# Attention: transposing the row maxima and the sums as 64-row products on both halves of TensorE, into two shared PSUM banks

## Chip, cores, metric

One core of one Trainium2 chip runs the whole program. The metric is the device time of one execution in microseconds; the shown times are medians of several executions.

## The reference

Two layers A (sliding-window attention) and two layers B (a spectral filter: 2-D FFT, a product with complex weights, inverse FFT), in the order A, B, A, B, each on a layer-normalised input and with its residual added. The change lies in A alone:

```python
def _A_ref(x, wqkv, wo):            # x is (1, 2048, 576)
    B, S, D = x.shape
    H = 32; Dh = D // H; W = 256    # 32 heads of 18
    ...                             # q, k, v from x @ wqkv, per head
    scores = jnp.einsum("bhqd,bhkd->bhqk", q, k) * (Dh ** -0.5)
    idx = jnp.arange(S)
    mask = (idx[:, None] - idx[None, :] >= 0) & (idx[:, None] - idx[None, :] < W)
    scores = jnp.where(mask[None, None], scores, -1e9)
    p = _softmax(scores, axis=-1)
    o = jnp.einsum("bhqk,bhkd->bhqd", p, v)
    return (lambda x, *d: x.transpose(*d))(o, 0, 2, 1, 3).reshape(B, S, D) @ wo
```

Each query sees itself and the 255 keys before it. All values are 32-bit floats.

## The kernel before

The instructions of each engine run in the order in which the Python code issues them; semaphores between the engines are placed by the library from the tiles that instructions read and write.

Attention handles the 32 heads in 8 groups of 4 (`NQ = 8`), and the 2048 positions in 16 tiles of 128. A step `t` of the main loop (from -10 to 129 in each layer) is one tile of one group. `qs` and `ks_` hold the queries and keys of a group transposed: two heads (`hp`) in partitions 0 to 63 and 64 to 127, two more (`pair`) in a second plane. Row 63 of each half of `qs` holds minus the maximum of that query, against a row of ones in `ks_`, so that the product of all 64 rows gives score minus maximum.

- `score_max(x, pair, hp)`, ten steps ahead (`LEAD = 10`): PE multiplies 63 rows of q and k into a bank `S` (L811); DVE adds the mask and takes the maximum of each query into a column of `ms` (L813).
- `m_rows(n, c)`, once in four steps (t = 4k + 2): PE transposes the 16 columns of maxima of four tiles (L819, bank `tpm`), ACT negates them into `mt` (L821), and four DMAs on the queue of SP put them into row 63 of `qs`.
- `exps(x, pair, hp)`: PE multiplies 64 rows of k and q into a bank `E` (L843), ACT takes the exponential into `P` (L844), POOL cuts the window's edges (L846, L849).
- `pv(x)`, two steps behind: PE multiplies `P` with v, which has a nineteenth column of ones, into `U` (L863): 19 rows for each head, starting at partitions 0, 32, 64 and 96, the last of them the sum of the exponentials. After four tiles ACT copies `U` to `us` (L868).
- `norm(n, c)`, in the same steps as `m_rows` and right behind it: PE transposes the four 128-column blocks of `us` into one bank `tpo` (L873), DVE takes the reciprocals of the sums (L876) and multiplies (L878) into `o`, which a DMA stores.
- `proj` makes q and k of later groups from the input, 14 pairs of 64-row products of 512 columns for each block of 128 rows and 512 positions (L750), one of a pair on each half of the array, spread over the steps; ACT copies one result (L758), DVE adds the other (L762).

In a step PE's order is: E, E, S, S (first `pair`), the products of `pv`, E, E, S, S (second `pair`), some products of `proj`, and in every fourth step `m_rows` and `norm`.

PSUM has eight banks: `U`, two for `proj`, and five for all else. `bank(name)` gives those five: a counter `turns` runs over the calls from t = 0 on, and its value modulo 5 decides between tag `S` (three banks: 1, 2, 0) and tag `E` (two banks: 3, 4). A new tile can be written once the readers of an earlier tile in the same bank are done. Before t = 0 only tag `S` is used.

After attention the object `out` multiplies with `wo`. There a tile `tpl` of one bank is used in slices of 128 columns, one for each tile of positions: `turn_last` transposes into a slice (L511), `split_last` reads it with ACT (L516) and then with DVE (L517). Slices 0, 1, 2 are written together and read in turn; later slice 3 is written and read, and then slice 0 is written again.

Of the kernel before, what the change touches and what calls it, by code (L numbers as in the profile page):

```python
# [8 lines left out]
F32 = mybir.dt.float32  # L9
F32R = mybir.dt.float32r  # L10
BF = mybir.dt.bfloat16
AF = mybir.ActivationFunctionType
# [563 lines left out]
def layer_a(tc, src, dst, wqk_d, wv_d, wo_d, dc_d, gc_d, dram, copy, wvs, wos, second, spectral):  # L576
    nc = tc.nc
    V, A, T, P = nc.vector, nc.scalar, nc.tensor, nc.gpsimd
# [7 lines left out]
    with ExitStack() as ctx:  # L586
        cp = ctx.enter_context(tc.tile_pool(name="ac", bufs=1))
        ident = cp.tile([128, 128], F32, name="ident")
# [127 lines left out]
        with ExitStack() as c2:  # L716
            wp = c2.enter_context(tc.tile_pool(name="a2", bufs=2))
# [56 lines left out]
            def bank(name):  # L774

                turns[0] += t >= 0
                return pp.tile([128, 512], F32, name=name, **(dict(tag="E", bufs=2) if turns[0] % 5 > 2 else dict(tag="S", bufs=3)))
# [3 lines left out]
            def stack_load(n, c):  # L781

                q, k = qs[n % 2], ks_[n % 2]
                cs = slice(c * 512, c * 512 + 512)
                for which, t, parts in ((0, q, (0, 0, 1)), (1, k, (0, 1, 0))):
                    for hp in range(2):
                        r0 = 144 * n + 72 * which + 36 * hp
                        for slot, part in enumerate(parts):
                            b = 64 * hp + 18 * slot
                            nc.sync.dma_start(t[b:b + 18, :, cs].bitcast(F32),  # L790
                                              qk_d[part, r0:r0 + 36, cs].rearrange("(f d) t -> d f t", f=2).bitcast(F32))

            def v_load(n):
                v = wp.tile([128, NT, 4, 19], F32, tag="vq", name=f"vq{n}", bufs=2)
                nc.sync.dma_start(v.rearrange("p b h e -> p (b h e)"), v_d[n].rearrange("p b e -> p (b e)"))
                vts[n] = v

            ms = {}

            def score_max(x, pair, hp):  # L800

                n, i = divmod(x, NT)
                c, t = divmod(i, 4)
                q, k = qs[n % 2], ks_[n % 2]
                if t == hp == pair == 0:
                    ms[n, c] = wp.tile([128, 2, 2, 4], F32, tag="m", name=f"m{n}_{c}", bufs=3)
                lo, hi = max(0, i - 2) * 128, (i + 1) * 128
                N = hi - lo
                b = 64 * hp
                ps = bank(f"S{x}_{pair}_{hp}")  # L810
                T.matmul(ps[:, 0:N], q[b:b + 63, pair, i * 128:i * 128 + 128], k[b:b + 63, pair, lo:hi], start=True, stop=True)  # L811
                jk = wp.tile([128, 384], BF, tag="jk", name=f"jk{x}_{pair}_{hp}", bufs=3)
                V.tensor_tensor_reduce(out=jk[:, 0:N], in0=ps[:, 0:N], in1=mask[:, 384 - N:384], scale=1.0, scalar=-3e38,  # L813
                                       op0=ALU.add, op1=ALU.max, accum_out=ms[n, c][:, hp, pair, t:t + 1])

            def m_rows(n, c):
                q = qs[n % 2]
                tp = bank(f"tpm{n}_{c}").rearrange("p (a t) -> p a t", a=4)
                T.transpose(tp[0:16, 0], ms[n, c].rearrange("p a b t -> p (a b t)"), ident)  # L819
                mt = wp.tile([16, 128], F32R, tag="mt", name=f"mt{n}_{c}", bufs=2)  # L820
                A.activation(mt, tp[0:16, 0], AF.Copy, scale=-1.0)  # L821
                for hp in range(2):
                    for pair in range(2):
                        r = (hp * 2 + pair) * 4
                        b = 64 * hp + 63
                        nc.sync.dma_start(q[b:b + 1, pair, c * 512:c * 512 + 512].rearrange("a (t q) -> a t q", t=4).bitcast(F32),
                                          mt[r:r + 4].bitcast(F32))
# [24 lines left out]
            us = {}  # L852
# [14 lines left out]
                    us[n, i // 4] = u = wp.tile([128, 512], F32, tag="us", name=f"us{n}_{i}", bufs=1)  # L867
                    A.copy(u, U)  # L868

            def norm(n, c):  # L870
                tp = bank(f"tpo{n}_{c}").rearrange("p (a t) -> p a t", a=4)
                for a in range(4):
                    T.transpose(tp[:, a], us[n, c][:, a * 128:a * 128 + 128], ident)  # L873
                tv = tp.rearrange("p a (h e) -> p (a h) e", e=32)
                rc = wp.tile([128, 16, 1], F32, tag="rc", name=f"rc{n}_{c}", bufs=2)
                V.reciprocal(rc, tv[:, :, 18:19])  # L876
                o = wp.tile([128, 4, 72], F32, tag="o", name=f"o{n}_{c}", bufs=2)
                V.tensor_mul(o.rearrange("p a (h e) -> p (a h) e", e=18), tv[:, :, 0:18], rc.to_broadcast([128, 16, 18]))  # L878
                lo, hi = 72 * n, 72 * n + 72
                for a, f0, f1 in ((o_d, 0, 448), (o7_d, 448, 576)):  # L880
                    b, e = max(lo, f0), min(hi, f1)
                    if b < e:
                        nc.sync.dma_start(a[c * 512:(c + 1) * 512, b - f0:e - f0].rearrange("(a p) e -> p a e", a=4), o[:, :, b - lo:e - lo])
# [10 lines left out]
            NX = NQ * NT  # L894
            LEAD = 10
# [4 lines left out]
            for m in range(22):  # L900
                a, b = [2 + 23 * z // 5 for z in (m, m + 1)]
# [6 lines left out]
            for t in range(-LEAD, NX + 2):  # L908

                if t + LEAD in (0, 2):  # L910
                    stack_load(0, 2 + (t + LEAD) // 2)
                n, c = divmod(t + 20, NT)
                if c % 4 == 0 and 0 < n < NQ:
                    stack_load(n, c // 4)
                if t + LEAD == 5:
                    v_load(0)
                if t + 12 in range(NT, NX, NT):
                    v_load((t + 12) // NT)

                want = goal.get(t, len(pj))  # L920
                more, done = pj[done:want], want
                for pair in range(2):
                    for hp in range(2):
                        if 0 <= t < NX:
                            exps(t, pair, hp)
                    for hp in range(2):
                        if t + LEAD < NX:
                            score_max(t + LEAD, pair, hp)
                    while later:
                        later.pop()()  # L930
                    if pair == 0 and 0 <= t - 2 < NX:
                        pv(t - 2)
                    if pair == 0 and t < 2:
                        for f in more[:(len(more) + 1) // 2]:
                            f()
                        more = more[(len(more) + 1) // 2:]
                for f in more:
                    f()
                if copy and t >= 32 and t % 4 == 0 and t < 32 + 16 * len(copy):

                    z, r = divmod(t // 4 - 8, 4)
                    P.dma_start(*[a[32 * r:32 * r + 32] for a in copy[z]])

                y = t + LEAD - 1
                if 0 <= y < NX and y % 4 == 3:
                    m_rows(*divmod(y // 4, 4))
                y = t - 3
                if 0 <= y < NX - 1 and y % 4 == 3:
                    norm(*divmod(y // 4, 4))
                if t == OB - 16:  # L950
                    out.room()
                if t - OB in (0, 1, 2):
                    out.load(t - OB)
                if t == OB + 3:
                    out.consts()
                    out.last(slice(96, 128), slice(0, 56))
                if t == NX - 1:
                    out.last(slice(0, 96), slice(0, 128))

                if t - OB - 4 in (0, 1, 2, 4):  # L960
                    out.tail(min(t - OB - 4, 3))
                if t - OB - 5 in (0, 1, 2):
                    u = t - OB - 5
                    out.turn(u, pp.tile([128, 512], F32, tag="pj", name=f"tpa{u}", bufs=2), V)
                    if u < 2:
                        out.load(u + 3)
                if t == NX:

                    A.activation(wp.tile([128, 1], F32, name="se", bufs=1), eps, AF.Sqrt)
            out.early(0, [pp.tile([128, 512], F32, tag="S", name=f"ops0_{n}", bufs=3) for n in range(2)], slice(0, 4))  # L970

            for k in range(4):
                tp = pp.tile([128, 512], F32, tag="E" if k in (1, 2) else "pj", name=f"tpz{k}", bufs=2)[0:32]
                for a in range(4):
                    T.transpose(tp[:, 128 * a:128 * a + 128], us[NQ - 1, 3][:, 4 * k + a:512:16], ident)
                tv = tp.rearrange("p (a h e) -> p a h e", a=4, h=4)
                rc = wp.tile([128, 4, 4, 1], F32, tag="rc", name=f"rcz{k}", bufs=2)[0:32]
# [5 lines left out]
            tp = pp.tile([128, 512], F32, tag="pj", name="tpl", bufs=2)  # L983
# [47 lines left out]
```

## Time and profile before

| | |
|---|---|
| median of 3 runs | 1542.78 us (1542.71 to 1547.83) |
| the profiled execution | 1542.73 us, span of its instructions 1540.7 us |
| granted TensorE clock, mean | 0.966 of full speed |
| busy, PE | 1403.2 us, 91% of the span |
| busy, DVE | 962.1 us, 62% |
| busy, ACT | 815.6 us, 53% |
| busy, POOL | 726.1 us, 47% |
| L819 (maxima, PE) | 64 of 280 ns |
| L873 (sums, PE) | 248 of 275 ns |
| L821 (ACT) | 64 of 263 ns |
| L876, L878 (DVE) | 62 of 256 ns, 62 of 457 ns |

In a row of a group or of the timeline, `out<-in` are the tiles by their names in the program, `64*128` after a PE product are the rows and columns of the array that it uses, and then the shape written and the shape read follow. PE is the matmul, PEld the load of its stationary operand. In the timeline the first number is the start in us from the span's start, the second the time from the first start to the last end of the x instructions; in brackets stands the idle time of the engine ahead of them and what ended it. Matmuls are pipelined: one that takes 0.28 us may be followed by the next after 0.11.

### The profile page before, as it was taken

The numbers are of one execution on the slowest core, as the hardware profiler recorded it, in microseconds if no ns is written. First come the engines' busy times: TensorE is split into PE (matmuls) and PEld (weight loads), VectorE is DVE, ScalarE is ACT, GpSimd is POOL, SyncE is SP. The second block draws the span as 40 slices with busy tenths as digits, with TensorE's granted clock in tenths as the row PEclk, the third lists the DMA queues.
The fourth block names the chain that finished last, engine by engine and source line by source line (L and its number), as shares of the span: only waits on it lengthen the run. The fifth ranks groups of instructions, "written<-read, shape, count | busy, mean of one in ns | idle before, by whom it ended". The sixth has DMA issues, their size and how long they took to land. (4 is left out here: it accounts for less than half of the span.)

```text
span 1540.7 us, 35484 instructions
## 1 busy us (share of the span) xinstructions
PE 1403.2 (91%) x12312; PEld 1071.6 (70%) x12312; DVE 962.1 (62%) x3103; ACT 815.6 (53%) x1895; POOL 726.1 (47%) x1215
## 2 busy tenths in 40 slices
PE   7997999999999899877789979999999998998677
PEld 7985666666656798537689856666666567985376
DVE  5356787788884555445443567878888835554445
ACT  6523767677666444225455236777666654442254
POOL 3364566566544333244611646565555443332445
PEclk9998999999999999988989989999999999999889
DMA  7856456555555366666374565555445553656663
GB/s 235 266 172 213 151 166 183 165 169 160 158 166 151 123 219 199 224 198 203 135 226 114 178 212 152 163 157 155 147 140 156 158 150 119 223 191 224 194 207 135
DMA packets 197423, 271.81 MB, mean 176 GB/s; under 512 B 87294, under 2 KB 109438, under 8 KB 196030
## 3 DMA queue, kind: packets, MB, share of 16 engines
q1 hardware_dynamic: 185502, 250.65, 52.3%
q10 hardware_dynamic: 10976, 15.59, 3.0%
q0 software_dynamic: 768, 3.31, 0.8%
q8 instruction: 99, 1.62, 0.5%
q14 instruction: 78, 0.64, 0.1%
HBM read 167.88 MB, written 103.86 MB: 176 GB/s over the span
## 5 line engine op out<-in xcount | busy, mean ns | idle before, releaser
L813 DVE CUSTOM_DVE_ANT_0 jk<-S,mask 128x384 bf16<-128x384 f32 (+2 forms) x1024 | 500.0, 529 | 111.5 <-PE S L811 106.9
L844 ACT ACTIVATE P<-E 128x384 f32<-128x384 f32 (+2 forms) x1024 | 423.2, 476 | 187.2 <-PE E L843 157.0
L846 POOL TENSOR_SCALAR_AFFINE_SELECT P<-P 128x512 f32<-128x512 f32 x256 | 162.3, 634 | 295.2 <-ACT P L844 277.8
L843 PE MATMUL E<-qs,ks 64*128 64x384 f32 (+2 forms) x1024 | 233.2, 400 | 21.8 <-DMA qs<-mt 15.3
L811 PE MATMUL S<-ks,qs 63*128 63x384 f32 (+2 forms) x1024 | 234.2, 367 | 3.3 <-DMA wqr<-in_wqk 1.9
L863 PE MATMUL U<-P,vq 128*19 128x128 f32 (+1 forms) x3840 | 202.9, 329 | 1.0 <-POOL P L849 1.0
L843 PEld LDWEIGHTS E<-qs,ks 64*128 64x128 f32 x1024 | 123.9, 184 | 106.2 <-issue 44.3
L750 PE MATMUL pj<-xh,wqh 64*128 64x512 f32 (+1 forms) x640 | 165.9, 405 | 2.1 <-ACT vt L710 1.7
L811 PEld LDWEIGHTS S<-ks,qs 63*128 63x128 f32 x1024 | 130.8, 186 | 44.8 <-ACT P L844 20.3
L863 PEld LDWEIGHTS U<-P,vq 128*19 128x19 f32 x3840 | 89.9, 98 | 93.5 <-issue 34.5
L849 POOL TENSOR_SCALAR_AFFINE_SELECT P<-P 128x512 f32<-128x512 f32 x224 | 142.0, 634 | 0.0
L750 PE MATMUL pj<-xl,wqh 64*128 64x512 f32 (+1 forms) x512 | 128.4, 395 | 0.0
L750 PE MATMUL pj<-xh,wql 64*128 64x512 f32 (+1 forms) x640 | 120.6, 392 | 0.0
L522 PE MATMUL ops<-oroom 128*128 128x288 f32 x784 | 113.7, 301 | 4.4 <-DVE oroom L505 3.0
L522 PEld LDWEIGHTS ops<-oroom 128*128 128x128 f32 x784 | 106.6, 191 | 6.2 <-DVE oroom L505 4.0
L171 POOL TENSOR_TENSOR eo<-xn 128x287 f32<-128x287 f32 x32 | 26.1, 817 | 148.2 <-ACT xn L169 148.2
L750 PEld LDWEIGHTS pj<-xh,wqh 64*128 64x128 f32 (+1 forms) x640 | 88.0, 188 | 7.4 <-ACT vt L710 2.1
L813 DVE DVE_READ_ACCUMULATOR2_ANT m<- 128x1 f32 x1024 | 85.0, 83 | 0.0
L199 PE MATMUL pf<-dc,et 128*128 128x290 f32 x384 | 72.4, 313 | 9.6 <-DVE et L190 6.5
L750 PEld LDWEIGHTS pj<-xh,wql 64*128 64x128 f32 (+1 forms) x640 | 72.2, 186 | 7.7
L764 POOL TENSOR_TENSOR sg<-sg 128x512 fp32r<-128x512 f32 x56 | 72.0, 1286 | 4.7
L750 PEld LDWEIGHTS pj<-xl,wqh 64*128 64x128 f32 (+1 forms) x512 | 71.3, 189 | 3.7
(181 smaller groups left out, 2555.4 us busy)
## 6 DMA issues: line engine op xcount, KB each, us to landing
qk_d<-sg SPq DMA_DIRECT2D x56, 512.0 KB
qs<-qk_d SPq DMA_DIRECT2D x384, 72.0 KB
ks<-qk_d SPq DMA_DIRECT2D x384, 72.0 KB
v_d<-vt SPq DMA_DIRECT2D x32, 304.0 KB
vq<-v_d SPq DMA_DIRECT2D x16, 608.0 KB
yd<-ye SPq DMA_DIRECT2D x32, 290.0 KB
wt<-in_w SPq DMA_DIRECT2D x16, 580.0 KB
x<-ofree SPq DMA_DIRECT2D x32, 288.0 KB
```

The source lines that it names most:

```text
L171: P.tensor_add(eo[:, 0, 1:288], xn[:, 1:288], xn[:, 575:288:-1])
L199: T.matmul(o, et[:, c, si], m(5 * c + mi), start=q == 0, stop=False)
L522: self.nc.tensor.matmul(self.ps[u][n][:, 0:288], x, self.w[p][:, wk * D + n * 288:wk * D + n * 288 + 288], start=first and i == 0, stop=la ...
L750: T.matmul(ps, w[r, wk], xT(xk, cs)[r], start=s == 0, stop=s == len(ks) - 1)
L764: (P if halves else V).tensor_sub(sg[:, 1], su, sg[:, 0].bitcast(F32))
L811: T.matmul(ps[:, 0:N], q[b:b + 63, pair, i * 128:i * 128 + 128], k[b:b + 63, pair, lo:hi], start=True, stop=True)
L813: V.tensor_tensor_reduce(out=jk[:, 0:N], in0=ps[:, 0:N], in1=mask[:, 384 - N:384], scale=1.0, scalar=-3e38, op0=ALU.add, op1=ALU.max, accu ...
L843: T.matmul(ps[:, 0:nq], k[b:b + 64, pair, j * 128:j * 128 + 128], q[b:b + 64, pair, j * 128:j * 128 + nq], start=True, stop=True)
L844: A.activation(p[:, hl_, 0:nq], ps[:, 0:nq], AF.Exp, scale=SC)
L846: P.affine_select(out=p[:, :, 0:128], in_=p[:, :, 0:128], pattern=[[0, 4], [1, 128]], compare_op=ALU.is_ge, fill=0.0, base=0, channel_mult ...
L849: P.affine_select(out=p[:, :, 256:384], in_=p[:, :, 256:384], pattern=[[0, 4], [-1, 128]], compare_op=ALU.is_gt, fill=0.0, base=0, channel ...
L863: T.matmul(U[32 * h:32 * h + 19, (q0 % 4) * 128:(q0 % 4) * 128 + 128 * (q1 - q0)], vts[n][:, j, h], pt[n, j][:, h, (q0 - j) * 128:(q1 - j) ...
```

## The change

`m_rows` and `norm` get two banks, `tps`, taken together ahead of both, in place of one bank each. Each transposition of 128 rows becomes two of 64 rows, of partitions 0 to 63 into the first bank and of partitions 64 to 127 into the second. The maxima go to columns 256 to 319 of both banks, the sums (heads 0 and 1 in the first bank, 2 and 3 in the second) to columns 0 to 255. ACT's copy of the maxima, DVE's reciprocal and DVE's product become two instructions each, one for each bank, in the order shown. A block at t = 4k + 2 takes both banks also where only one of the two parts is due.

```diff
-            def m_rows(n, c):
+            halves = (slice(0, 64), slice(64, 128))
+
+            def m_rows(n, c, tps):
                 q = qs[n % 2]
-                tp = bank(f"tpm{n}_{c}").rearrange("p (a t) -> p a t", a=4)
-                T.transpose(tp[0:16, 0], ms[n, c].rearrange("p a b t -> p (a b t)"), ident)
+                for tp, r in zip(tps, halves):
+                    T.transpose(tp[0:16, 256:320], ms[n, c].rearrange("p a b t -> p (a b t)")[r], ident[r, r])
                 mt = wp.tile([16, 128], F32R, tag="mt", name=f"mt{n}_{c}", bufs=2)
-                A.activation(mt, tp[0:16, 0], AF.Copy, scale=-1.0)
+                for tp, r in zip(tps, halves):
+                    A.activation(mt[:, r], tp[0:16, 256:320], AF.Copy, scale=-1.0)
...
-            def norm(n, c):
-                tp = bank(f"tpo{n}_{c}").rearrange("p (a t) -> p a t", a=4)
+            def norm(n, c, tps):
                 for a in range(4):
-                    T.transpose(tp[:, a], us[n, c][:, a * 128:a * 128 + 128], ident)
-                tv = tp.rearrange("p a (h e) -> p (a h) e", e=32)
-                rc = wp.tile([128, 16, 1], F32, tag="rc", name=f"rc{n}_{c}", bufs=2)
-                V.reciprocal(rc, tv[:, :, 18:19])
+                    for tp, r in zip(tps, halves):
+                        T.transpose(tp[:, 64 * a:64 * a + 64], us[n, c][r, a * 128:a * 128 + 128], ident[r, r])
+                tvs = [tp[:, 0:256].rearrange("p (a h e) -> p a h e", a=4, e=32) for tp in tps]
+                rcs = [wp.tile([128, 4, 2, 1], F32, tag=f"rc{g}", name=f"rc{n}_{c}_{g}", bufs=2) for g in range(2)]
                 o = wp.tile([128, 4, 72], F32, tag="o", name=f"o{n}_{c}", bufs=2)
-                V.tensor_mul(o.rearrange("p a (h e) -> p (a h) e", e=18), tv[:, :, 0:18], rc.to_broadcast([128, 16, 18]))
+                for tv, rc in zip(tvs, rcs):
+                    V.reciprocal(rc, tv[:, :, :, 18:19])
+                for g, (tv, rc) in enumerate(zip(tvs, rcs)):
+                    V.tensor_mul(o[:, :, 36 * g:36 * g + 36].rearrange("p a (h e) -> p a h e", e=18), tv[:, :, :, 0:18],
+                                 rc.to_broadcast([128, 4, 2, 18]))
...
-                y = t + LEAD - 1
-                if 0 <= y < NX and y % 4 == 3:
-                    m_rows(*divmod(y // 4, 4))
-                y = t - 3
-                if 0 <= y < NX - 1 and y % 4 == 3:
-                    norm(*divmod(y // 4, 4))
+                if t % 4 == 2 and t > -LEAD:
+                    y, z = t + LEAD - 1, t - 3
+                    tps = [bank(f"tp{t}_{g}") for g in range(2)]
+                    if y < NX:
+                        m_rows(*divmod(y // 4, 4), tps)
+                    if z >= 0:
+                        norm(*divmod(z // 4, 4), tps)
```

## The prediction

> **What bounds the kernel now.** I read the page first (its group rows), then the busy time in the two attention stretches, the waits of PE, and the timeline around one of the edited places. The edited code runs in the attention loop. Two windows of 290 us, one in each attention layer (columns: stretch, its length, then busy us and count for PE, PEld, DVE, ACT, POOL, granted clock, DMA share, GB/s):
>
> ```profile
> 160.00:450.00 290.00, 287.68 (x3114) 188.21 (x3112) 233.03 (x903) 202.17 (x493) 173.92 (x259) 1.00 0.56 169
> 928.00:1218.00 290.00, 287.67 (x3110) 188.22 (x3112) 233.01 (x904) 202.52 (x493) 165.67 (x244) 1.00 0.52 157
> ```
>
> PE is busy 99% of both, DVE 80%, ACT 70%, at a granted clock of 1.00. PE hardly waits here; the largest wait of the steady loop in the list of PE's waits is
>
> ```profile
> PE E L843 <- ACT P L844: 5.1, 19, 0.4
> ```
>
> 5.1 us over both layers. So whatever PE loses or gains at an edited place goes to the end nearly whole. PE around one such place (t = 4k+2, where `m_rows` and `norm` stand together), filtered to PE:
>
> ```profile
> 305.34 0.40 PE L750 MATMUL pj<-xl,wqh 64*128 64x512 f32 x2
> 305.57 0.40 PE L750 MATMUL pj<-xh,wqh 64*128 64x512 f32 x2
> 305.90 0.28 PE L819 MATMUL tpm<-ident,m 128*16 128x128 f32 x1
> 306.01 0.60 PE L873 MATMUL tpo<-ident,us 128*128 128x128 f32 x4
> 306.54 0.44 PE L843 MATMUL E<-qs,ks 64*128 64x384 f32 x2
> 306.82 0.33 PE L811 MATMUL S<-ks,qs 63*128 63x384 f32 x2
> 307.08 0.39 PE L863 MATMUL U<-P,vq 128*19 128x256 f32 x1
> ```
>
> Two 64-row projection products run side by side every 0.23 us (305.34 to 305.57), but the 128-row transposition after them starts 0.33 later. The four of `norm` start 0.11 apart (0.60 for all, of which the last takes 0.27), so the last starts at 306.34; the 64-row E pair follows 0.20 later, and S 0.28 after E. Where E and S follow other 64-row products, both steps are shorter:
>
> ```profile
> 309.24 0.33 PE L843 MATMUL E<-qs,ks 64*128 64x384 f32 x2
> 309.41 0.33 PE L811 MATMUL S<-ks,qs 63*128 63x384 f32 x2
> ```
>
> 0.17 from E to S. Entering and leaving the 128-row form thus costs about 0.1 + 0.1 + 0.1 us. The Trainium skill, TensorEngine Tiling, section Tiling Modes, Key Properties, says that a change of the tiling mode drains TensorE; these rows agree.
>
> **The order of accesses to one bank.** The change lets a maxima block and a sums block share the same two banks, ACT reading columns 256 to 319 and PE then writing columns 0 to 255. What the program does in such a case stands at the end of the attention, in tile `tpl`, whose 128-column slices are used one by one:
>
> ```profile
> 498.37 0.27 ACT L516 CAST oroom<-tpl 128x128 fp32r<-128x128 f32 x1 [7.48 <-PE tpl L511]
> 498.99 0.27 ACT L516 CAST oroom<-tpl 128x128 fp32r<-128x128 f32 x1 [0.36 <-DVE oroom L517]
> ```
>
> ```profile
> 498.67 0.29 DVE L517 TENSOR_TENSOR oroom<-tpl,oroom 128x128 fp32r<-128x128 f32 x1 [3.71 <-ACT oroom L516]
> ...
> 503.54 0.28 DVE L517 TENSOR_TENSOR oroom<-tpl,oroom 128x128 fp32r<-128x128 f32 x1
> ```
>
> ```profile
> 503.88 0.33 PE L511 MATMUL tpl<-ident,ofree 128*128 128x128 f32 x1 [0.49 <-DVE oroom L517]
> ```
>
> ACT's second read (columns 128 to 255) waits until DVE has read columns 0 to 127 (498.96). At 503.88 PE writes columns 0 to 127, which were finished with long before, yet waits for DVE's read of columns 384 to 511, done at 503.82. So accesses of different engines to one bank are put one after the other, whatever their columns, and a release takes 0.06 us. The Trainium skill, PSUM — Partial Sum Buffer, section Terms, calls two engines on one bank and quadrant at once a collision; that rule speaks against sharing a bank, the rows agree that it is avoided by waiting, and by it the sum below stands instead of that of the second rival.
>
> **The change, part by part.** Blocks with both parts: t = 6, 10, ... 118, 29 in a layer, 58 in all (62 `norm`, less two in each layer that stand alone). P = 0 is the last projection pair (305.57). Now: `tpm` 0.33, E 0.97, S 1.25, U 1.51.
>
> ACT and DVE in the same block:
>
> ```profile
> 305.12 0.87 ACT L844 ACTIVATE P<-E 128x384 f32<-128x384 f32 x2 [0.58 <-PE E L843]
> 306.21 0.27 ACT L821 ACTIVATE mt<-tpm 16x128 fp32r<-16x128 f32 x1 [0.22 <-PE tpm L819]
> 307.08 0.49 ACT L844 ACTIVATE P<-E 128x384 f32<-128x384 f32 x1 [0.60 <-PE E L843]
> ```
>
> ```profile
> 305.30 0.56 DVE L813 CUSTOM_DVE_ANT_0 jk<-S,mask 128x384 bf16<-128x384 f32 x1 [0.42 <-PE S L811]
> 305.78 0.08 DVE L813 DVE_READ_ACCUMULATOR2_ANT m<- 128x1 f32 x1
> ...
> 306.65 0.26 DVE L876 RECIPROCAL rc<-tpo 128x16 f32<-128x16 f32 x1 [0.31 <-PE tpo L873]
> 306.94 0.46 DVE L878 TENSOR_TENSOR o<-tpo,rc 128x288 f32<-128x288 f32 x1
> ```
>
> and the groups that give slopes by width:
>
> ```profile
> L294 DVE TENSOR_TENSOR ofree<-p,wt 128x580 f32<-128x580 f32 x32 | 24.4, 762 | 38.7 <-POOL uv L299 20.9 <-PE p L290 17.8
> ...
> L504 ACT CAST oroom<-tpo 128x512 fp32r<-128x512 f32 x22 | 12.9, 589 | 0.0
> ...
> L557 DVE RECIPROCAL ofree<-ofree 128x1 f32<-128x1 f32 x32 | 5.0, 157 | 3.6 <-ACT ofree L553 3.6
> ```
>
> 1. Maxima. The 64-row pair follows the projections without a switch: 0.23 instead of 0.33. Streaming 64 columns instead of 128 saves a quarter of the 0.11 pitch (load and stream are 128 columns each), 0.03, so ACT starts at 0.23 + 0.31 - 0.03 = 0.51. From L504 and `mt` ACT pays 0.84 ns a column, so a half takes 0.27 - 0.05 = 0.21. Two exponentials of 0.48 take 0.87, a pitch of 0.39 for 384 columns (0.32 of slope and 0.07), which gives 0.12 for 64. Both halves are read at 0.51 + 0.12 + 0.21 = 0.84. They now stand on the path: behind them PE waits.
>
> 2. Sums. The first transposition into each bank must wait for ACT's read there: the second bank's starts at 0.90, with its load at 0.95. Behind the waiting product PE's whole queue stands. Eight products of 64 rows replace four: a pair costs 0.08 if the halves load side by side (0.055 load, 0.03 stream) and 0.165 if one after the other; no row shows it, I take 0.11, between them and today's pitch. The last pair starts at 0.95 + 3 x 0.11 = 1.28, E at 1.33, the first S at 1.50.
>
> 3. DVE. The last transposition of the first bank is seen after 0.31 - 0.03 = 0.28 (306.34 to 306.65 today): 1.56. Order in the queue: reciprocal, reciprocal, product, product. Reciprocal of 8 columns: 157 + 7/15 of 100 = 0.20. Product: L294 and the 0.46 give 1.04 ns a column, so 144 columns take 0.31. Successive DVE instructions start 0.07 before the end of the one ahead (0.56 long, next after 0.48), so the first product ends 0.13 + 0.13 + 0.31 = 0.57 later, at 2.13. The DVE total (0.72 to about 0.9 a block) would alone be covered by its 20% of idle time.
>
> 4. The banks come back later. Five banks go round: after the two of the block follow E, E, S, S, and the second S takes the fifth, the maxima bank. That today's maxima bank is what it waits for shows where ACT is late:
>
> ```profile
> 260.51 0.40 PE L750 MATMUL pj<-xh,wql 64*128 64x512 f32 x2
> ...
> 261.76 0.50 PE L811 MATMUL S<-ks,qs 63*128 63x384 f32 x2
> 262.19 0.41 PE L863 MATMUL U<-P,vq 128*19 128x256 f32 x4
> ```
>
> ```profile
> 261.05 0.60 ACT L758 COPY sg<-pj 128x512 f32<-128x512 f32 x1
> 261.51 0.26 ACT L821 ACTIVATE mt<-tpm 16x128 fp32r<-16x128 f32 x1
> ```
>
> The S pair takes 0.50 instead of 0.33: the second starts at 262.26 - 0.44 = 261.82, just behind `mt` (261.77), and U 0.37 behind it. Now `mt` frees that bank at 0.91 from P; afterwards it is the product of sums, 2.13, so the second S starts at 2.19 and U at 2.56. Another slot would have to come from the exponential of the new E, which ends about as late (it starts 0.54 behind E, 306.54 to 307.08: 1.33 + 0.54 + 0.49 = 2.36). Delay at U: 2.56 - 1.51 = 1.05 us.
>
> 5. Blocks with late ACT and DVE. Of 62 reciprocals 44 waited for PE:
>
> ```profile
>   PE tpo L873: 38.6, 44
> ```
>
> In the other 18 a projection's copy sits ahead. There `mt` starts at 1.00 from P (261.51), is read by 1.33, the last pair starts at 1.39 + 0.05 + 0.33 = 1.77, the first product of sums ends 2.62, U is at 3.05 against 1.68 today: 1.37. Today such a block pays later for the late DVE (the next S pair is held by about 0.3), which then has passed: about 1.07.
>
> 6. The other six maxima blocks and four sums blocks have no partner and wait for nothing new; the saved switch and the extra instructions I put at nothing. `bank` for t < 0 gives two of three S banks to a maxima block, held only for two reads of ACT; three blocks a layer at 0.1 would be under 1 us. The DMAs of `m_rows` are the same four, issued up to 0.5 us later, ten steps ahead of their use.
>
> **Sum.** 40 x 1.05 + 18 x 1.07 = 61 us. The profiled execution took 1542.73 us (span 1540.7), as good as the median of 1542.78: **1604 us**. Ends of the unknown: pairs at 0.08 or 0.165 (-0.09, +0.165), DVE without or with twice the overlap (-0.13, +0.13), ACT without overlap (+0.09), S to U in 0.26 (-0.11), together 0.72 to 1.44 a block: 1585 to 1627 us.
>
> **Rivals.** *Half the price:* only one of the two waits shows. If a free bank is there for the second S, E at 1.33, S pair at 1.50, U at 1.76: +0.25, 1557 us. If instead sums need not wait for ACT, the last pair starts at 0.62, the product ends 1.47, U at 1.90: +0.39, 1565 us. Against: both waits follow from rows above; for: the slots are dealt out by a planner, and it may find another order. *The switch decides, and the kernel gets faster:* without both waits the pairs start at 0.29, E at 0.67, S 0.84, U 1.10, which saves 0.41 a block, 24 us: 1519 us. It wins as soon as the waits add less than 0.41 a block; my sum has 1.05 + 0.41 = 1.46. For it speaks only the saved 0.3 of drains; against it `tpl`. *No change:* the delay is swallowed by waits that PE has anyway. 5.1 us of them are listed, so it needs nearly all of the 61 to vanish. *Worse:* later products wait for the second bank too, over 1627.
>
> **How the numbers follow.** A measurement of this kernel tells about 0.5% (8 us) from no change. Forecast 0.75, half the price 0.09, switch decides 0.08, no change 0.04, worse 0.04. Slower by over 0.5%: 0.75 + 0.09 + 0.04 = 0.88; faster 0.08; same 0.04. The likeliest alone: 1585 to 1627. For 8 in 10 the range takes in half the price: 1555 to 1628.
>
> **What would show it.** Right: `tp` of `norm` waits for ACT `mt`, 58 times, E starts about 0.4 us later after the last projection; the second S starts 0.06 behind the first of the two products that replace L878; PE's busy share in the attention falls by about a tenth; E to S 0.17 instead of 0.28. Wrong: E within 0.7 us of the last projection, or S pairs together with U 0.26 later. The prediction falls if ACT's and PE's accesses to these banks are not ordered, or if the second S finds a free bank.

## The result and the profile after

The changed kernel takes 1637.72 us, median of 4 runs (1633.59 to 1639.91); the kernel before took 1545.08 us on the same chip (1542.71 to 1547.83). The ratio is 1.0603, with a 95% interval of 1.0579 to 1.0628. The forecast had the direction and both waits; the time lies 34 us above it and 10 us above its range. Medians and ranges here and below are of all runs, while a ratio leaves out a run in which the core was slower than in its other runs (one of `x3_share_128`, 1633.71 us, and one of `x5_fill_late`, 1660.2 us at a clock of 0.828).

The two windows of attention, as in the first fence of the prediction (the second 44.5 us later, as the attention of that layer starts 44.5 us later), then the row of the granted clock from the page, in 40 slices, after and before:

```profile
160.00:450.00 290.00, 269.42 (x2948) 177.19 (x2942) 213.13 (x864) 183.44 (x468) 159.81 (x237) 0.97 0.49 150
972.50:1262.50 290.00, 268.74 (x2942) 177.02 (x2938) 212.92 (x864) 183.42 (x468) 151.69 (x221) 0.97 0.45 138
```

```profile
PEclk9998999989996999988989989999899569999989
```

```profile
PEclk9998999999999999988989989999999999999889
```

In equal time PE now does 2948 and 2942 products instead of 3114 and 3110, and its busy share is 93% instead of 99%. But the clock is no longer 1.00 either: 0.97 in the windows, and in the row of slices a 6, and a 5 and a 6, stand at the ends of the two attention layers, where the row of before has nines. Two things were lost, waits and clock. Of PE's list of waits, the rows that the change adds to the steady attention loop (us in all, times, longest):

```profile
PE tp L876 <- ACT mt L824: 23.5, 56, 0.9
...
PE S L811 <- DVE o L883: 17.4, 41, 0.8
...
PE S L811 <- ACT P L847: 4.5, 10, 0.5
```

Transpositions of the sums wait for ACT's read of the maxima, and S waits for DVE's product, more rarely for an exponential. One block on PE, and what ACT and DVE do in it (the last projection pair, 322.00, is P = 0):

```profile
322.00 0.40 PE L750 MATMUL pj<-xh,wqh 64*128 64x512 f32 x2
322.24 0.22 PE L821 MATMUL tp<-ident,m 64*16 64x64 f32 x2
322.76 0.50 PE L876 MATMUL tp<-ident,us 64*128 64x64 f32 x7 [0.30 <-ACT mt L824]
323.07 0.42 PE L846 MATMUL E<-qs,ks 64*128 64x384 f32 x1
323.10 0.22 PE L876 MATMUL tp<-ident,us 64*128 64x64 f32 x1
323.13 0.42 PE L846 MATMUL E<-qs,ks 64*128 64x384 f32 x1
323.33 0.34 PE L811 MATMUL S<-ks,qs 63*128 63x384 f32 x1
324.07 0.41 PE L811 MATMUL S<-ks,qs 63*128 63x384 f32 x1 [0.40 <-DVE o L883]
324.41 0.41 PE L866 MATMUL U<-P,vq 128*19 128x256 f32 x4
```

```profile
322.49 0.32 ACT L824 ACTIVATE mt<-tp 16x64 fp32r<-16x64 f32 x2
...
323.37 0.31 DVE L881 RECIPROCAL rc<-tp 128x8 f32<-128x8 f32 x2 [0.60 <-PE tp L876]
323.61 0.87 ACT L847 ACTIVATE P<-E 128x384 f32<-128x384 f32 x2 [0.80 <-PE E L846]
323.62 0.52 DVE L883 TENSOR_TENSOR o<-tp,rc 128x144 f32<-128x144 f32 x2
```

The two S products, which stood side by side, are 0.74 us apart, and everything else of PE stands behind the second.

To split the loss I compare, step for step, the distances between the first E products of every fourth step, so that each distance holds one of the 58 blocks, with those of before. All 58 together are longer by 95.9 us; the span grew by 96.9 (1540.7 to 1637.6). In 39 of them the clock stays at 1.00: median +0.85 us, mean +0.91. The other 19 touch a stretch at half clock and are longer by 60.6 us. So the waits cost about 58 x 0.85 = 49 us (53 by the mean), and the rest of 95.9, 43 to 46 us, comes in the blocks at half clock. "A block" below means this median over blocks at full clock, "all blocks" the sum over 58. Both are of the one execution that was profiled; that of `x1_late_read`, `x2_no_sum_reads` and `x7_ahead_of_proj` is 7 to 9 us faster than the median given with it.

### The profile page after: what moved, and what is told of

Read it like the earlier page. It is cut to its first block, busy times and chain, and to the rows that moved or that the text cites. A ratio compares the mean times of both kernels' runs of the same rounds, so it can differ in the third digit from the quotient of the medians.

```text
span 1637.6 us, 36486 instructions
## 1 busy us (share of the span) xinstructions
PE 1457.1 (89%) x12624; PEld 1099.1 (67%) x12624; DVE 968.1 (59%) x3227; ACT 820.9 (50%) x1959; POOL 726.3 (44%) x1215
## 5 line engine op out<-in xcount | busy, mean ns | idle before, releaser
L811 PE MATMUL S<-ks,qs 63*128 63x384 f32 (+2 forms) x1024 | 262.9, 390 | 25.9 <-DVE o L883 17.4
L846 PE MATMUL E<-qs,ks 64*128 64x384 f32 (+2 forms) x1024 | 250.4, 427 | 19.4 <-DMA qs<-mt 16.4
L866 PE MATMUL U<-P,vq 128*19 128x128 f32 (+1 forms) x3840 | 224.2, 356 | 0.8 <-POOL P L852 0.8
L846 PEld LDWEIGHTS E<-qs,ks 64*128 64x128 f32 x1024 | 136.8, 202 | 101.8 <-issue 49.6
L811 PEld LDWEIGHTS S<-ks,qs 63*128 63x128 f32 x1024 | 144.0, 200 | 81.6 <-PE S L811 31.1
L866 PEld LDWEIGHTS U<-P,vq 128*19 128x19 f32 x3840 | 94.7, 103 | 106.7 <-issue 53.4
```

The lines of the kernel that those rows point to most:

```text
L846: T.matmul(ps[:, 0:nq], k[b:b + 64, pair, j * 128:j * 128 + 128], q[b:b + 64, pair, j * 128:j * 128 + nq], start=True, stop=True)
L866: T.matmul(U[32 * h:32 * h + 19, (q0 % 4) * 128:(q0 % 4) * 128 + 128 * (q1 - q0)], vts[n][:, j, h], pt[n, j][:, h, (q0 - j) * 128:(q1 - j) ...
```

## The experiments

**Reading the maxima later.** In `x1_late_read` the block puts all ten transpositions ahead of ACT's reads:

```diff
                     if y < NX:
                         m_rows(*divmod(y // 4, 4), tps)      # the transpositions alone
                     if z >= 0:
+                        norm_t(*divmod(z // 4, 4), tps)      # the transpositions alone
+                    if y < NX:
+                        m_read(*divmod(y // 4, 4), tps)      # ACT's reads, DMAs
+                    if z >= 0:
                         norm(*divmod(z // 4, 4), tps)
```

> The changed kernel, with all ten transpositions of a block issued ahead of ACT's two reads of the maxima, so that PE no longer waits for ACT before the sums. Theory (two waits, and a clock that falls with them): the wait for ACT, 0.3 us a block in the trace of after, goes, but DVE now comes behind ACT's read of the same bank, so the second S is only about 0.3 us earlier: 17 us less from that, and fewer stretches at half clock, 10 to 30 us less: 1590 to 1615 us. Rival 1 (the 64-row form itself, 16 loads in place of 5, is what costs): no change, 1633 to 1640. Rival 2 (only the order of DVE's four instructions holds PE): 1630 to 1640.

1574.06 us (1567.24 to 1581.62), ratio 1.018 (1.0114 to 1.0247): less than expected. PE in a block, and its wait:

```profile
312.57 0.40 PE L750 MATMUL pj<-xh,wqh 64*128 64x512 f32 x2
312.81 0.21 PE L821 MATMUL tp<-ident,m 64*16 64x64 f32 x2
312.87 0.41 PE L879 MATMUL tp<-ident,us 64*128 64x64 f32 x8
313.09 0.42 PE L849 MATMUL E<-qs,ks 64*128 64x384 f32 x2
313.40 0.44 PE L811 MATMUL S<-ks,qs 63*128 63x384 f32 x1
314.25 0.41 PE L811 MATMUL S<-ks,qs 63*128 63x384 f32 x1 [0.41 <-DVE o L888]
```

```profile
PE S L811 <- DVE o L888: 18.2, 32, 1.4
```

The first wait is gone from the list, E follows 0.52 after the last projection instead of 1.07, and the ten transpositions run 0.06 a pair. The second wait stays. A block costs 0.45 instead of 0.85, and only one of 58 still touches half clock: all blocks +28.4 us. The mean clock of the four runs is 0.955 to 0.970, against 0.928 to 0.935 after the change. Removing one wait of 0.4 a block (23 us) won 64 us in the median.

**Nobody reads the sums.** `x2_no_sum_reads` leaves out DVE's reciprocals and products; the output tile is set to a constant by POOL, so the division is not computed:

```diff
-                for tv, rc in zip(tvs, rcs):
-                    V.reciprocal(rc, tv[:, :, :, 18:19])
-                for g, (tv, rc) in enumerate(zip(tvs, rcs)):
-                    V.tensor_mul(o[:, :, 36 * g:36 * g + 36]...
+                P.memset(o, 0.5)
```

> The changed kernel without DVE's two reciprocals and two products: o is filled with a constant by POOL, so the division by the sums is left out of the result. The banks are then free after ACT's read. Theory: the second S no longer waits (0.6 to 0.7 us a block), the wait for ACT stays (0.3): 58 x 0.65 = 38 us less, and without long gaps the clock stays up, another 30 to 45: 1555 to 1575 us. Rival 1 (the 64-row form costs): 1625 to 1640, since DVE was not the limit. Rival 3 (the wait for ACT is the main part): 1615 to 1630.

1569.64 us (1560.24 to 1575.17), ratio 1.0144 (1.0077 to 1.0212), as expected. A block costs 0.17, all blocks +17.3 us. The other wait stands alone and as long as before:

```profile
PE tp L876 <- ACT mt L824: 23.6, 56, 1.0
```

So either wait alone leaves the clock nearly up: the runs here have 0.954 to 0.965, those of before beside them 0.958 to 0.970, and 4 of 58 blocks touch half clock. The run also spares DVE about 1 us of work a block (two reciprocals of 0.19 and two products of 0.30), so it does not part the bank from DVE's load; the row S <- DVE `o` after the change names the bank's reader.

**The same sharing with 128 rows.** `x3_share_128` keeps the two shared banks but transposes with all 128 rows, as before the change: the maxima into the first bank, the sums two and two:

```diff
-                for tp, r in zip(tps, halves):
-                    T.transpose(tp[0:16, 256:320], ms[n, c]...[r], ident[r, r])
+                T.transpose(tps[0][0:16, 256:384], ms[n, c]..., ident)
...
                 for a in range(4):
-                    for tp, r in zip(tps, halves):
-                        T.transpose(tp[:, 64 * a:64 * a + 64], us[n, c][r, a * 128:a * 128 + 128], ident[r, r])
+                    T.transpose(tps[a // 2][:, a % 2 * 128:a % 2 * 128 + 128], us[n, c][:, a * 128:a * 128 + 128], ident)
```

> The sharing alone: two banks taken together for maxima and sums as in the change, but every transposition with 128 rows (maxima in columns 256 to 383 of the first bank, two blocks of sums in each). Theory: the waits come with the sharing, not with the halves; PE pays the switches again (E about 0.2 later), the second S waits for the first product of sums as in after: 1630 to 1650 us. Rival 1 (the 64-row form costs): back to 1545 to 1560.

1624.06 us (1606.43 to 1633.71), ratio 1.0465 (1.0373 to 1.0556): slightly below the expectation, far above the rival's. A block costs 1.03, and PE waits at the same place:

```profile
320.15 0.28 PE L820 MATMUL tp<-ident,m 128*16 128x128 f32 x1
...
320.79 0.66 PE L873 MATMUL tp<-ident,us 128*128 128x128 f32 x4 [0.36 <-ACT mt L822]
321.38 0.44 PE L844 MATMUL E<-qs,ks 64*128 64x384 f32 x2
321.67 0.77 PE L811 MATMUL S<-ks,qs 63*128 63x384 f32 x2
```

```profile
PE tp L873 <- ACT mt L822: 27.1, 58, 0.9
```

The S pair takes 0.77 instead of 0.33: the second starts at 322.03, 0.15 behind the end of DVE's first product, as after the change. The sharing costs without any 64-row transposition; with them a block is 0.18 cheaper (0.85). The four runs differ in the clock: the fastest, 1606.43 us, had 0.970, as much as the kernel before, and is 63 us above the median of that kernel beside it (1543.28), close to the waits alone (58 x 1.03 = 60); the profiled one, 1625.94, had 0.946. The same waits can thus go with or without the loss of clock.

**Separate banks.** `x4_own_banks` returns the maxima to a bank of their own with 128 rows and keeps the sums as halves in two banks:

```diff
-                    tps = [bank(f"tp{t}_{g}") for g in range(2)]
                     if y < NX:
-                        m_rows(*divmod(y // 4, 4), tps)
+                        m_rows1(*divmod(y // 4, 4))       # as before the change
                     if z >= 0:
-                        norm(*divmod(z // 4, 4), tps)
+                        norm(*divmod(z // 4, 4), [bank(f"tp{t}_{g}") for g in range(2)])
```

> The 64-row sums without sharing: the maxima as before the change (128 rows, a bank of their own), the sums in halves into two banks that hold nothing else, so three banks a block. Theory: no wait for ACT; the second S still waits for DVE's product, as in the kernel with late reads (0.45 us a block there), and one switch more is paid, 0.2 to 0.3: 1575 to 1595 us, clock as before. Rival (the halves are free and sharing alone costs): 1530 to 1545.

1594.74 us (1589.84 to 1602.73), ratio 1.0316 (1.0256 to 1.0375), at the upper edge of the expectation. No transposition waits for ACT; the second S does for DVE:

```profile
PE S L811 <- DVE o L896: 22.5, 50, 1.1
```

A block costs 0.61, all blocks +47.3 us; in the second layer the clock is at half for 20.5 us, which the expectation did not have. Three of five banks are now held ahead of E, E, S, S, so the second S still comes back to a bank that DVE reads.

**The clock at the end of a layer.** Both long stretches of half clock lie in the steps without projections, which end the attention of a layer (the second begins 1 us ahead of them); the last four blocks of the second layer are longer by 6.1, 5.6, 4.4 and 5.8 us. Two experiments go there. `x6_old_late` has the change up to step 103 and the form before from step 104; `x5_fill_late` keeps the change everywhere and adds work that nobody reads, two pairs of 64-row products of 512 columns in each of steps 104 to 122:

```diff
+                    if t < 104:
                         tps = [bank(f"tp{t}_{g}") for g in range(2)]
...
+                    else:                                 # x6: as before the change
+                        m_rows1(...), norm1(...)
```

```diff
+                if 104 <= t <= 122:                       # x5
+                    kk = ks_[t // NT % 2]
+                    for f in range(2):
+                        if f == 0:
+                            fl = [pp.tile([128, 512], F32, tag="pj", ...) for g in range(2)]
+                        for ps, r in zip(fl, halves):
+                            T.matmul(ps, kk[r, 0, 0:128], kk[r, 1, 0:512], start=f == 0, stop=f == 1)
```

> The changed kernel up to step 103 of each layer; from step 104 on, where no projection products are left, m_rows and norm as before the change (128 rows, a bank each). Theory (the clock is granted by PE's activity, and the last steps fall under what it asks): the half-clock stretches of 37 and 65 us go, and the late blocks, which cost 14 and 22 us in after, cost nothing: 1598 to 1606 us. Rival (a cost of 0.9 us in every block and a clock that has other reasons): 8 x 0.9 = 7 us less, 1627 to 1633.

> The changed kernel with idle work added: in each step from 104 to 122 of a layer two more pairs of 64-row products of 512 columns, into banks that nothing reads (0.46 us a step, 17 us over both layers where nothing covers them). All waits stay. Theory (the clock falls because PE does too little in the last steps): the stretches at half clock in the last steps go, 36 us of late blocks become 7, and at most 17 are added: 1610 to 1628 us, faster with more work. Rival (the late blocks are long because no projection is there to run behind the waits, and the clock only follows): 1640 to 1655.

`x6_old_late`: 1604.41 us (1603.19 to 1605.61), ratio 1.0378 (1.031 to 1.0447). `x5_fill_late`: 1614.45 us (1612.54 to 1660.2), ratio 1.0433 (1.0385 to 1.048). Both as expected, and neither interval touches that of the change (1.0579 to 1.0628). Eight of the 58 blocks returned to the old form give back 33 us, where eight times 0.85 would be 7; and more work is faster than less. The added work does not hide the waits: those for ACT `mt` and DVE `o` are still 23.4 us (58 times) and 19.7 us (45 times). The same stretch of time after the change, and with the added products:

```profile
478.00:520.00 42.00, 39.84 (x291) 20.87 (x290) 21.37 (x86) 21.12 (x57) 13.48 (x22) 0.56 0.19 56
```

```profile
478.00:520.00 42.00, 39.07 (x468) 23.76 (x464) 22.14 (x90) 30.14 (x80) 20.48 (x36) 1.00 0.30 80
```

291 products at a clock of 0.56 against 468 at 1.00. In the second layer step 104 starts at 1276.1 us after the change and at 1200.4 before. The 20 us ahead of it and the steps behind it, after and then before:

```profile
1255.00:1275.00 20.00, 17.79 (x195) 11.45 (x197) 14.76 (x62) 13.58 (x34) 11.41 (x18) 1.00 0.45 137
1275.00:1340.00 65.00, 62.96 (x434) 33.00 (x426) 32.95 (x134) 31.31 (x80) 19.21 (x32) 0.50 0.26 81
```

```profile
1180.00:1200.00 20.00, 19.84 (x207) 13.01 (x205) 15.36 (x63) 14.35 (x35) 11.21 (x18) 1.00 0.55 160
1200.00:1250.00 50.00, 46.77 (x492) 25.41 (x495) 33.33 (x130) 36.82 (x94) 24.99 (x41) 1.00 0.43 132
```

PE is busy for 89% instead of 99% of the 20 us, and then the clock is at half for the whole stretch, 434 products in 65 us instead of 492 in 50. In `x6_old_late` and `x5_fill_late` PE is busy for 89% of the 20 us ahead of step 104 as well (17.79 of 20), and the clock drops there too, but it comes back: in the second layer after 13.7 us and 3.4 us, where the change stays down for 64.9. The two differ from the change only from step 104 on, so the work behind the drop decides how long it lasts.

**A place with shelter.** Two attempts to make a version that wins. `x7_ahead_of_proj` reads late, as `x1_late_read`, and moves the block ahead of the rest of the step's projections (from step 104, old form and place), so that they cover the waits. `x8_behind_pv` is the kernel before with its 128-row maxima and sums moved right behind the 128-row products U, so that one change of form serves both:

```diff
+                if t % 4 == 2 and -LEAD < t < 104:        # x7: the block
+                    ...
                 for f in more:                            # the projections left in the step
                     f()
```

```diff
                     if pair == 0 and 0 <= t - 2 < NX:
                         pv(t - 2)
+                    if pair == 0:                         # x8: moved here from the step's end
+                        m_rows(...), norm(...)
```

> Late reads, and the block moved ahead of the step's projection products, so that three or four pairs of them (0.7 to 0.9 us) run while DVE frees the banks; from step 104 on the form of before. Theory (only the wait for the banks costs, the halves themselves save 0.4 to 0.5 us a block): 50 blocks save 0.2 to 0.5: 1518 to 1533 us. Rival 1 (the halves cost): over 1550. What can spoil it: the reads of the banks now stand behind two exponentials on ACT and two maxima on DVE, so the second S may still wait 0.3.

> The kernel before with m_rows and norm (128 rows, a bank each) moved right behind the products of pv, where PE leaves the 128-row form anyway. Theory of the switches (about 0.3 us around a block): one exit is shared, 0.2 to 0.3 x 62 = 12 to 19 us less: 1524 to 1533 us. If the later reads on ACT and DVE hold banks: 1540 to 1560.

`x7_ahead_of_proj`: 1556.04 us, median of 10 (1548.35 to 1563.88), ratio 1.0055 (1.0026 to 1.0085). Much better than the change, but not faster than before, where 1518 to 1533 was expected. The list of PE's waits shows a new one:

```profile
PE tp L821 <- ACT P L850: 11.9, 36, 0.5
```

The two old waits are gone but for 0.7 us; the block itself now finds no bank, since an exponential still reads it. A block costs 0.18, all blocks +11.6 us, none of them at half clock. `x8_behind_pv`: 1539.86 us, median of 10 (1536.29 to 1542.62), ratio 0.9956 (0.9938 to 0.9975), 7 us below the kernel before in the median (1547.12 beside it), where I expected 12 to 19. That is less than the 0.5% that the prediction sets for a measurement, and its trace does not place it: all blocks together are 1.8 us shorter than before. A block there:

```profile
303.53 0.85 PE L863 MATMUL U<-P,vq 128*19 128x256 f32 x16
304.31 0.28 PE L819 MATMUL tpm<-ident,m 128*16 128x128 f32 x1
304.42 0.60 PE L873 MATMUL tpo<-ident,us 128*128 128x128 f32 x4
304.95 0.44 PE L843 MATMUL E<-qs,ks 64*128 64x384 f32 x2
305.23 0.34 PE L811 MATMUL S<-ks,qs 63*128 63x384 f32 x2
```

Between U and the projections there is no other change of form any more, but leaving this one costs what it did: E 0.64 behind the maxima (306.54 - 305.90 before), S 0.28 behind E. In steps 8 to 99 the step with the block is 3.19 us long in the median instead of 3.29, and the one behind it 2.55 instead of 2.48; why the second takes back most of the gain stays open.

**Neither wait.** `x9_neither_wait` joins `x1_late_read` and `x2_no_sum_reads` (the division is left out again), to see what the 64-row form itself is worth:

> Late reads, and DVE's reciprocals and products left out (o is filled with a constant by POOL, the division by the sums is left out of the result): the halves with neither wait. Theory: what is left is the saving of the switches and of the side by side transpositions, 0.4 us in 58 blocks, 23 us, with the clock as before: 1515 to 1528 us. Rival 1 (the halves cost by themselves): 1545 or more.

1541.08 us, median of 10 (1534.55 to 1550.39), ratio 0.997 (0.9939 to 1.0001). This form costs nothing, but its gain, if any, is far below the 1515 to 1528 us that I expected. A block:

```profile
304.91 0.39 PE L750 MATMUL pj<-xh,wqh 64*128 64x512 f32 x2
305.14 0.22 PE L821 MATMUL tp<-ident,m 64*16 64x64 f32 x2
305.20 0.41 PE L879 MATMUL tp<-ident,us 64*128 64x64 f32 x8
305.42 0.42 PE L849 MATMUL E<-qs,ks 64*128 64x384 f32 x2
305.74 0.61 PE L811 MATMUL S<-ks,qs 63*128 63x384 f32 x2
```

```profile
305.74 0.35 PEld L811 LDWEIGHTS S<-ks,qs 63*128 63x128 f32 x2 [0.16 <-DVE m L813]
```

E comes 0.51 after the last projection instead of 0.97, but S comes 0.32 behind E instead of 0.17, and its pair takes 0.61: DVE's maxima hold the banks next. The saving of the switches is there at first: in steps 8 to 99 the step that ends with the block is shorter than before by 0.46 us in the mean, but the next one is longer by 0.29. A block saves 0.19, not 0.41. The steps at the end of the second layer again touch half clock for 13.7 us, so all blocks of this execution (1547.1 us) save only 0.2 us in sum.

## Why the prediction came out as it did

The chain of waits held step by step, with the size of one term off, and one term was missing.

1. *Maxima.* 0.23, ACT from 0.51, both halves read at 0.84. Measured in the block shown: 0.24, 0.49, 0.81 (322.49 + 0.32).

2. *Sums.* The second bank's first at 0.90, the last pair at 1.28, E at 1.33, the first S at 1.50. Measured: about 0.86, between 1.04 and 1.10, 1.07 and 1.33. The wait is right, and `x1_late_read` removes it alone. The pitch of the pairs is mis-sized: I took 0.11 between bounds of 0.08 and 0.165; `x1_late_read` has eight products in 0.41, of which one lasts 0.22, so (0.41 - 0.22) / 3 = 0.06, below my lower bound. The pairs come faster than load and stream were put at there. So E starts 0.10 later than before, not the 0.4 that was to show the forecast right, and S follows E after 0.26, where 0.17 was to be seen.

3. *DVE.* First product ends at 2.13, 0.57 behind the first reciprocal. Measured, by the records of the single instructions, 1.37 to 1.92: 0.55.

4. *Banks come back later.* The second S at 2.19, U at 2.56. Measured 2.07 and 2.41. The second S waits for DVE's product, which `x2_no_sum_reads` confirms by taking it away; its release took 0.15 here where I put 0.06. Delay at U: 1.05 expected, 2.41 - 1.51 = 0.90 measured.

5. *Late blocks* (1.07) and the sum: a block at full clock costs 0.85 in the median. For the waits this gives 49 us instead of 61; the pitch is the larger part of the difference.

6. *The clock: the step that failed.* The prediction read "at a granted clock of 1.00" from the windows of before and kept it for after, without a reason. It did write that PE's busy share "falls by about a tenth" (from 99 to 93%), but nowhere asked what that does to the clock: the sum has no term for it, and no rival either. The runs put 43 to 46 us there: with the waits' 49 to 53 that is the 96 us of the blocks. Of these, 29 us lie in the last four blocks of each layer (35.8 us, less 8 x 0.85), and for them `x6_old_late` and `x5_fill_late` show that they are tied to how dense PE's work is at the ends of the layers, where no projections fill it. The others lie in twelve earlier blocks with short stretches at half clock, for which no run was made. `x1_late_read` and `x2_no_sum_reads` show that it takes both waits: with either alone the clock stays nearly up. With 49 us for the waits the sum would have given 1592; the rest of the 1637.72 goes with the clock.

Of the rivals, *half the price* is refuted, since both waits show. Alone, they cost 0.17 (`x2_no_sum_reads`) and 0.45 (`x1_late_read`) a block, where that rival had 0.25 and 0.39. Counted from `x9_neither_wait`, whose block is 0.19 shorter than before, the wait for ACT adds 0.36 and the wait for DVE 0.64; together that is 1.00, and the change stands at 0.85 + 0.19 = 1.04. So the two waits are nearly the whole of it, and nearly additive in blocks at full clock. *The switch decides* is refuted for the change and half true of its mechanism: without both waits `x9_neither_wait` is 0.3% below before, in an interval that just reaches no change, where that rival's 0.41 a block gave 1519 us. The saved switches are there (E 0.51 instead of 0.97 after the projection), but the next step takes more than half of them back. *No change* falls with the interval. *Worse* came out in time (over 1627), though by a mechanism it did not name.

The statement on `tpl`, accesses of different engines to one bank put in order whatever their columns, carried over: PE writes the columns of the sums only after ACT has read those of the maxima, with 56 waits after the change, 56 in `x2_no_sum_reads` and 58 in `x3_share_128`. The order is made by the program's semaphores; no run here lets the two accesses meet.

What stays open is which quantity trips the clock. No gap of PE in the 20 us ahead of the two long drops is over 0.40 and 0.72 us. The busy share in front separates the change (89%) from before (99%), but `x5_fill_late` and `x6_old_late` have the same 89% and recover; and in `x1_late_read` the steps from 104 run at full clock with a share of 91%:

```profile
1223.00:1270.00 47.00, 42.93 (x458) 23.20 (x450) 33.27 (x137) 31.62 (x85) 21.78 (x36) 1.00 0.37 112
```

A few points of a busy share with modelled ends are no threshold, and once down, the change stays down at 97% busy (62.96 of 65). That share cannot be held against one at full clock, since a product then takes longer: 434 in 65 us are 6.7 per us, where before has 9.8.

## What to carry to other kernels

In this program, two pieces of work that different engines read cost an order of accesses when they share a bank, however far apart their columns are: count the new waits by bank, and follow the next pieces of work round the banks until one finds a free one. Where PE is the bound, add a term for the clock whenever a change thins PE's work, and look first at the stage with the least spare work to fill it; here a second wait of 0.4 us, 58 times, cost 23 us as a wait and about 40 more with the clock. A saving in one place of such a round is worth only what the next wait leaves of it.

## What the runs showed of the hardware

The granted clock fell to half without any long stop of PE: in the 20 us ahead, no gap was over 0.72 us before a stretch of 64.9 us at 0.50, which ran on with PE 97% busy by its modelled ends. Before the change the clock was at half for 103 us of the span, in attention only for 10.2 us at the start of each layer; after, for 233 us, in attention in stretches of 3.4, 6.8 and 10.2 us and two long ones of 37.5 and 64.9. The Trainium skill, TensorE: Matmul & The Clock Gate, section Part 1, has a window of about 3.4 us and only a half and a full setting, and these stretches agree. Its rule that the clock is full again after one such window of sustained work, and the advice there to avoid idle gaps over about 3.4 us, do not describe this drop: the gaps were shorter, and work that kept PE 97% busy at half clock did not bring it back for 19 windows.

A pair of transpositions of 64 rows on the two halves, which together do the work of one of 128 rows, went every 0.06 us against 0.11: in this size the halves reach almost double the rate, if nothing makes them wait.
